# Sigmoid attention with a SiLU MLP behind it: PSUM as three double tiles and two single banks in the stages that run attention under out products

## The chip, the cores and the metric

The kernel runs on one core of a Trainium2 chip. Its engines work side by side, each through its own list of instructions in order: TensorE (PE; its weight loads are listed apart as PEld), VectorE (DVE), ScalarE (ACT), GpSimd (POOL) and SyncE (SP, which here only issues transfers). They wait for each other through semaphores. Matrix products land in PSUM, eight banks of 512 float32 values in each of 128 partitions. The metric is the device time of one execution in microseconds.

## The reference

```python
def _attn_ref(q, k, v):                      # (8, 12, 448, 64) each
    S = q.shape[2]
    scale = 1.0 / np.sqrt(q.shape[-1])
    scores = scale * np.matmul(q, k.transpose(0, 1, 3, 2)) - np.log(S)
    attn = 1.0 / (1.0 + np.exp(-scores))
    return np.matmul(attn, v).astype(np.float32)

def _moe_ref(x, w_in, w_out):                # x (3584, 768), w_in (768, 2048), w_out (2048, 768)
    h = x @ w_in
    g = h * (1.0 / (1.0 + np.exp(-h)))
    return (g @ w_out).astype(np.float32)

def reference(**kwargs):
...
    attn_out = _attn_ref(**attn_kwargs)
    B, H, S, D = attn_out.shape
    x = np.ascontiguousarray(attn_out.transpose(0, 2, 1, 3)).reshape(B * S, H * D)
    return _moe_ref(x=x, **moe_kwargs)
```

The attention is a sigmoid of each score, with no sum over a row, so the scores of one piece of keys can be used as soon as they are there.

## The kernel before

**Attention.** A group g is two pairs of heads of one batch element; there are three groups to a batch element (NQ = 3) and 24 in all. A unit is one seventh of a group's keys (NCH = 7). `scores` (L209) makes one unit: eight half products (L216) into a PSUM tile psc of two banks, from the pool "double", and one ACT sigmoid over both banks (L223) into attnT in SBUF. `values` (L231) multiplies the seven attnT of a group with v (L245) into two banks pav, and DVE scales them into xT (L256). xT is the input of the first product of the MLP.

**First product, h.** For the first pair of batch elements `h_unit` (L273) makes h directly. For the later pairs `h_pair` (L348) makes it by seven products in place of eight of half the size (L364, tiles pa, pb, pc, pd), with sums that DVE and ACT make; the results go through SiLU on ACT (L358) into gTr. The sums of xT that it needs are made by `x_sums` (L334, four DVE subtractions L341 to L344), two thirds of them behind the fifth whole group of a stage (`after_values`, L646).

**Second product, out.** `out_set` (L473) makes the rows of two blocks with seven products po of eight matmuls each (L490), one bank each. DVE reads each po once or twice into the output rows osb (L500 to L525), and makes the sums S between them. `sets` (L556) strings the out_sets of one pair m together and yields after each matmul.

**Stages.** The loop over m (L747, m = 0, 1, 2) has two parts. In the first, attention of the next pair of batch elements runs under the out products of pair m: `burst` (L722) makes two units, and `values` of a group if one is waiting; then some matmuls of po follow, `many` behind a burst of scores alone, `few` (2 for m = 0 and 2, 4 for m = 1) behind one with values. m = 0 and 2 have three out_sets for 21 bursts, m = 1 has four. 14 po matmuls stand ahead of the bursts, and the last 8 behind them. In the second part `h_pair` makes h of the pair whose attention is now there. Ahead of the loop the first two batch elements go through attention and `h_unit`; behind it the last four out_sets run alone.

The order is written out by hand: each engine runs its instructions in the order in which the program calls them, on PE psc, psc, pav, po and so on.

**PSUM.** In the attention parts the eight banks are two pools: two tiles of two banks ("double", for psc) and four of one ("single", for everything else, pav and po among them). A pool hands out its tiles in turn, and a new tile waits until the work on the one that had its place is done. In h_pair every bank is a tile of its own, taken in the order of `ring` (L74): the singles first, longest idle ahead, then the banks of the doubles. `banks_for_attention` (L65) and `banks_for_h` (L74) switch between the two.

Of the kernel before, what the change touches and what calls it, by code (L numbers as in the profile page):

```python
# [11 lines left out]
F32 = mybir.dt.float32  # L12
# [5 lines left out]
def kernel(  # L18
# [14 lines left out]
    P = 128  # L33
# [19 lines left out]
    ctx.enter_context(tc.manual_schedule())  # L53

    psum = ctx.enter_context(ExitStack())
    banks, taken = {}, []
    NBANK, NDOUBLE = 8, 2
    NSINGLE = NBANK - 2 * NDOUBLE

    def new_pool(name, bufs):  # L60
        banks[name] = psum.enter_context(
            tc.tile_pool(name=name, bufs=bufs, space=bass.MemoryType.PSUM, reuse_waits="tile")
        )

    def banks_for_attention():  # L65
        psum.close()
        banks.clear()
        taken.clear()
        new_pool("double", NDOUBLE)
        new_pool("single", NSINGLE)  # L70

    ring = []

    def banks_for_h():  # L74
        oldest = len(taken) % NSINGLE
        ring[:] = [2 * NDOUBLE + (oldest + i) % NSINGLE for i in range(NSINGLE)]
        ring.extend(range(2 * NDOUBLE))
        psum.close()
        banks.clear()
        new_pool("any", 1)  # L80
        for i in range(NBANK):
            banks[i] = banks["any"].tile([P, 512], F32, tag=f"any{i}", name=f"any{i}")

    def one_bank(name):
        if "any" in banks:
            ring.append(ring.pop(0))
            return banks["any"].tile([P, 512], F32, tag=f"any{ring[-1]}", name=name)
        taken.append(name)
        return banks["single"].tile([P, 512], F32, tag="single", name=name)

    banks_for_attention()

# [113 lines left out]

    def scores(g, ch):  # L209
        attnT[g, ch] = p12.tile([P, 2, S], F16, tag="attnT", name="attnT")  # L210
        psc = banks["double"].tile([P, 2, 512], F32, tag="double", name="psc")
        for half in range(2):
            own = slice(half * HP, (half + 1) * HP)
            for j in range(2):
                rows = slice(j * D, (j + 1) * D)
                nc.tensor.matmul(  # L216
                    psc[own, j, :S],
                    qkT["k", g][rows, ch, own],
                    qkT["q", g][rows, :, own],
                    start=True,  # L220
                    stop=True,
                )
        nc.scalar.activation(attnT[g, ch], psc[:, :, :S], AF.Sigmoid, bias=bias_s, scale=QKSCALE)  # L223
# [5 lines left out]
    part_of = {}  # L229

    def values(g, end=NCH):  # L231
        b, iq = divmod(g, NQ)
        if b not in xT:
            assert b < 2 or b - 2 in h_done
            xT[b] = p2.tile([P, NPAIR, S], F16, tag="xT", name="xT")
        pav, done_rounds = part_of.pop(g, None) or (
            [one_bank("pav") for _ in range(2)],
            0,
        )
        for ch in range(done_rounds, end):  # L240
            at = attnT.pop((g, ch))
            for half in range(2):
                own = slice(half * HP, (half + 1) * HP)
                for j in range(2):
                    nc.tensor.matmul(  # L245
                        pav[half][j * D : (j + 1) * D, :S],
                        flat["v", g][own, j, ch, :],
                        at[own, j, :],
                        start=(ch == 0),
                        stop=(ch == NCH - 1),  # L250
                    )
        if end < NCH:
            part_of[g] = pav, end
            return
        for half in range(2):
            nc.vector.tensor_scalar_mul(xT[b][:, half * NQ + iq, :], pav[half][:, :S], SX)  # L256
        if iq == NQ - 1:
            ready.add(b)
# [75 lines left out]
    def x_sums(m, lo, hi):  # L334
        if lo == 0:
            for i in (1, 2, 4):
                tx[m, i] = room_x()
        of = slice(lo, hi)
        x0, x1 = ([xT[2 * m + j][:, c * NQ : (c + 1) * NQ] for c in range(2)] for j in range(2))
        sub = nc.vector.tensor_sub  # L340
        sub(tx[m, 1][:, of], x1[0][:, of], x0[0][:, of])  # L341
        sub(tx[m, 2][:, of], x1[1][:, of], tx[m, 1][:, of])
        sub(x1[0][:, of], x1[1][:, of], x1[0][:, of])
        sub(tx[m, 4][:, of], x0[1][:, of], tx[m, 2][:, of])  # L344
# [211 lines left out]
    def sets(m):  # L556
        for g in range(0, NCH - 1, 2):
            step = out_set(
                block(m, g), row_blocks(m, g), block(m, g + 1), row_blocks(m, g + 1)
            )  # L560
            for i, ns in enumerate(step):
                if m == 0 and g == 0 and i in (10, 14):
                    next(sums)
                if m == 0 and g == 0 and i in (20, 28, 36, 44):
                    next(in_sums)
                yield ns
        if m % 2 == 1:
            g = NCH - 1
            yield from out_set(
                kept, row_blocks(m - 1, g), block(m, g), row_blocks(m, g), m == B // 2 - 1  # L570
            )
# [3 lines left out]
    def rows_if_any(before, copy):  # L575
        if later and later[0][0] < before:
            g, name = later.pop(0)
            dma_transpose(g, name, copy)
            if name == "q":
                behind_rows(g, before)  # L580
# [48 lines left out]
    def after_values(g):  # L629
        if g == 0:  # L630
            load("v", 3)
            load_w_in(2)
            load_w_in(3)
        elif g == 1:
            load("v", 4)
            load_w_out(0, 0)
            load_w_out(0, 1)
        elif g == 2:
            load("v", 5)
            load_w_out(1, 0)  # L640
            load_w_out(1, 1)
            load("kq", 6)
            load("kq", 7)
        elif g + 3 < NQB:
            load("v", g + 3)
        if g >= 2 * NQ and g % (2 * NQ) == 2 * NQ - 2:  # L646
            x_sums(g // (2 * NQ), 0, NQ - 1)

    def values_if_any():
        if waiting:  # L650
            g = waiting.pop(0)
            values(g)
            after_values(g)
            return True
        return False
# [15 lines left out]
    def rounds(g, end):  # L671
        values(g, end)
        if end == NCH:
            after_values(g)
# [47 lines left out]
    def burst(n):  # L722

        new = units[n : n + 2]
        for u in new:
            scores(*u)
        with_values = values_if_any()
        for g, ch in new:
            if ch == NCH - 1:
                waiting.append(g)  # L730
                if 9 <= g + 3 < NQB:
                    later.extend(((g + 3, "k"), (g + 3, "q")))
        return with_values
# [11 lines left out]

    ENDING, FIRST_DENSE = 8, 14
    for m in range(B // 2 - 1):  # L747
        if m > 0:
            banks_for_attention()
        nc.scalar.activation(warm, bias_s, AF.Sigmoid)  # L750
        stream = sets(m)
        for _ in range(FIRST_DENSE):
            next(stream)

        dense = (3 + m % 2) * 7 * NHC - FIRST_DENSE - ENDING
        with_values = 2 * NQ - 1
        few = 2 + 2 * (m % 2)
        many = (dense - with_values * few) / (NT_B - with_values)
        own = 2 * NQ * (m + 2)
        behind_burst = 0.0  # L760
        for n in range(2 * NT_B * (m + 1), 2 * NT_B * (m + 2), 2):
            behind_burst += few if burst(n) else many
            rows_if_any(own, nc.vector.tensor_copy)
            half = int(behind_burst) // 2
            for i in range(int(behind_burst)):
                next(stream)
                if i == half:
                    rows_if_any(own, nc.vector.tensor_copy)
            behind_burst -= int(behind_burst)
        nc.scalar.activation(warm, bias_s, AF.Silu)  # L770
        for _ in stream:
            pass
        (g,) = waiting
        waiting.clear()
        banks_for_h()
        values(g, NCH - 1)

        def last_values():
            values(g)
            after_values(g)  # L780
            x_sums(m + 1, NQ - 1, NQ)
            nc.gpsimd.tensor_copy(gate, tx[m + 1, 4][:1, NQ - 1, :1])

        for i, _ in enumerate(h_pair(m + 1, last_values)):
            if i % 8 == 7:
                rows_if_any(NQB, nc.gpsimd.tensor_copy)
    banks_for_attention()
    for _ in sets(B // 2 - 1):
        pass

# [29 lines left out]
```

## Time and profile before

| | us |
|---|---|
| median of 3 runs | 375.46 (375.2 to 375.9) |
| the profiled execution | 375.68 |
| its span, first to last instruction | 373.7 |

| engine | busy us | share of the span | instructions |
|---|---|---|---|
| PE | 363.9 | 97% | 3009 |
| PEld | 182.4 | 49% | 3009 |
| DVE | 252.2 | 67% | 458 |
| ACT | 251.3 | 67% | 339 |
| POOL | 77.4 | 21% | 116 |

| stage of the loop | from, us | to, us |
|---|---|---|
| m = 0, attention under out products | 76.0 | 125.6 |
| m = 0, h_pair | 125.6 | 160.7 |
| m = 1, attention under out products | 160.7 | 215.5 |
| m = 1, h_pair | 215.5 | 250.6 |
| m = 2, attention under out products | 250.6 | 298.8 |
| m = 2, h_pair | 298.8 | 332.6 |

Times of the trace count from the first instruction. A row in order of time has the start, the time that the row covers, the engine, the line, the operation, what it writes and reads, and how many instructions were merged; in square brackets stands how long the engine was idle before, and what it waited for. Rows of one line that follow each other are merged, and matmuls overlap, so the time of a row is from its first start to its last end. A stage table has, after its bounds, its length, and then each engine's busy time and number of instructions.

### The profile page before, as it was taken

What the parts mean: (1) busy time and instruction counts of PE and PEld (TensorE: products, weight loads), DVE (VectorE), ACT (ScalarE), POOL (GpSimd) and SP (SyncE); (2) the same over time, 40 slices, a digit from 0 to 9 for tenths busy, and PEclk for the clock granted to TensorE, in tenths of its full rate; (3) what the DMA queues carried; (4) which work ended last, traced back from release to release, by engine and by line L of the source; (5) the groups of instructions that cost most, each with busy time, mean ns of one, the idle gap of its engine ahead of it and who ended that gap; (6) DMA issues with size and microseconds to landing.
All of it is one profiled execution on the core that took longest, in us unless ns stands there. A gap on an engine that the chain in (4) does not pass through costs nothing.

```text
span 373.7 us, 7596 instructions
## 1 busy us (share of the span) xinstructions
PE 363.9 (97%) x3009; PEld 182.4 (49%) x3009; DVE 252.2 (67%) x458; ACT 251.3 (67%) x339; POOL 77.4 (21%) x116
## 2 busy tenths in 40 slices
PE   7999999999999999999999999999999999999995
PEld 3554445544444455544444545544444545555553
DVE  2565469867655687867575758795655768797763
ACT  5998885479888756687777846679888946650000
POOL 8566521040051072000014046000100000000000
PEclk9999999999999999999999999999999999999999
DMA  8999999996769599008579669921964030003333
GB/s 133 201 204 204 204 204 204 166 142 128 124 107 210 117 129 172 18 0 128 107 137 165 142 129 134 109 37 28 171 97 97 2 87 0 3 0 84 86 84 84
DMA packets 65698, 42.78 MB, mean 114 GB/s; under 512 B 36096, under 2 KB 62208, under 8 KB 65664
## 3 DMA queue, kind: packets, MB, share of 16 engines
q0 software_dynamic: 27072, 22.58, 42.3%
q1 hardware_dynamic: 38240, 19.44, 27.1%
q8 instruction: 23, 0.38, 0.4%
q10 hardware_dynamic: 352, 0.30, 0.2%
q14 instruction: 11, 0.09, 0.1%
HBM read 45.61 MB, written 11.01 MB: 152 GB/s over the span
## 4 chain that ended last, share of the span: by engine, by line
PE 79%; DMA 9%; ACT 6%; issue 2%; DVE 2%; POOL 0%; ACTq 0%
PE po L490 31%; PE psc L216 9%; PE pa L364 7%; PE pav L245 7%; PE pc L364 7%; PE pd L364 7%; ACT attnT L223 5%; PE ph L277 5%; DMA kf<-in_k_dram 5%; PE pb L364 4%; DMA qf<-in_q_dram 2%; DMA w_in_sb<-in_moe_w_in_dram 2%; PE pw L174 2%; ACT gTr L358 1%; PE ptrq L187 1%
## 5 line engine op out<-in xcount | busy, mean ns | idle before, releaser
L223 ACT ACTIVATE attnT<-psc,bias_s 128x896 f16<-128x896 f32 x168 | 159.2, 1009 | 25.9 <-PE psc L216 25.5
L490 PEld LDWEIGHTS <-S 128*128 128x128 f16 x448 | 40.8, 98 | 36.3 <-issue 10.0
L216 PE MATMUL psc<-qT,kT 64*64 64x448 f16 x672 | 54.8, 364 | 3.0 <-ACT attnT L223 1.8
L256 DVE TENSOR_SCALAR xT<-pav 128x448 f16<-128x448 f32 x48 | 27.7, 620 | 32.5 <-PE pav L245 32.5
L115 POOL DMA_DIRECT2D vf<-in_v_dram x24 | 17.2, 716 | 135.6 <-PE pav L245 131.4
L490 PEld LDWEIGHTS <-gTr 128*128 128x128 f16 x336 | 30.8, 98 | 27.7 <-issue 9.7
L490 PE MATMUL po<-w_out_sb,gTr 128*128 128x384 f16 x224 | 42.5, 327 | 0.1
L490 PE MATMUL po<-T,S 128*128 128x384 f16 x224 | 42.5, 327 | 0.0
L364 PEld LDWEIGHTS <-w_in_sb 128*128 128x128 f16 x288 | 27.7, 98 | 26.9 <-issue 1.7
L490 PE MATMUL po<-w_out_sb,S 128*128 128x384 f16 x224 | 40.4, 327 | 0.0
L245 PE MATMUL pav<-attnT,vf 64*64 64x448 f16 x672 | 39.1, 350 | 0.5 <-DVE gTr L292 0.4
L277 PE MATMUL ph<-xT,w_in_sb 128*128 128x448 f16 x192 | 38.7, 353 | 0.1
L216 PEld LDWEIGHTS <-kT 64*64 64x64 f16 x672 | 17.9, 104 | 35.8 <-issue 32.2
L364 PE MATMUL pa<-xT,w_in_sb 128*128 128x448 f16 x144 | 33.2, 353 | 0.0
L364 PEld LDWEIGHTS <-SI 128*128 128x128 f16 x216 | 21.1, 98 | 20.0 <-issue 0.5
L245 PEld LDWEIGHTS <-vf 64*64 64x64 f16 x672 | 21.8, 106 | 12.8 <-issue 4.7
L277 PEld LDWEIGHTS <-w_in_sb 128*128 128x128 f16 x192 | 17.8, 98 | 19.1 <-issue 3.7
L380 ACT ACTIVATE part<-pa 128x448 f32<-128x448 f32 x24 | 13.1, 544 | 20.1 <-PE pa L364 19.2
L490 PE MATMUL po<-T,gTr 128*128 128x384 f16 x112 | 22.2, 327 | 0.0
L358 ACT ACTIVATE gTr<-pc 128x448 f16<-128x448 f32 x24 | 13.1, 544 | 12.9 <-DVE pc L374 12.5
L374 DVE TENSOR_TENSOR part<-pb,part 128x448 f32<-128x448 f32 x24 | 14.9, 621 | 8.3 <-ACT part L380 5.0
L177 ACT ACTIVATE m<-po 128x384 f32<-128x384 f32 x1 | 0.5, 492 | 27.7 <-PE po L490 27.7
(76 smaller groups left out, 468.4 us busy)
## 6 DMA issues: line engine op xcount, KB each, us to landing
out_dram<-osb SPq DMA_DIRECT2D x54, 192.0 KB, 3.0
vf<-in_v_dram POOLq DMA_DIRECT2D x24, 224.0 KB, 6.7
kf<-in_k_dram POOLq DMA_DIRECT2D x23, 224.0 KB, 7.6
qf<-in_q_dram POOLq DMA_DIRECT2D x23, 224.0 KB, 8.1
w_in_sb<-in_moe_w_in_dram POOLq DMA_DIRECT2D x16, 192.0 KB, 8.1
w_out_sb<-in_moe_w_out_dram POOLq DMA_DIRECT2D x4, 768.0 KB, 14.8
kT<-kr SPq DMA_TRANSPOSE x18, 4.1
qT<-qr SPq DMA_TRANSPOSE x18, 4.4
```

Source lines behind the costliest of these rows:

```text
L115: nc.gpsimd.dma_start(flat[name, g][:, :, c0:c1].rearrange("p i c d -> p i (c d)"), rows_in(name, g)[:, :, c0 * D : c1 * D],)
L174: nc.tensor.matmul(pw, dummy[:, :P], dummy, start=True, stop=True)
L216: nc.tensor.matmul(psc[own, j, :S], qkT["k", g][rows, ch, own], qkT["q", g][rows, :, own], start=True, stop=True,)
L223: nc.scalar.activation(attnT[g, ch], psc[:, :, :S], AF.Sigmoid, bias=bias_s, scale=QKSCALE)
L245: nc.tensor.matmul(pav[half][j * D : (j + 1) * D, :S], flat["v", g][own, j, ch, :], at[own, j, :], start=(ch == 0), stop=(ch == NCH - 1),)
L256: nc.vector.tensor_scalar_mul(xT[b][:, half * NQ + iq, :], pav[half][:, :S], SX)
L277: nc.tensor.matmul(ph[:, :S], w_in_sb[:, cc, fc * P : (fc + 1) * P], xT[b][:, cc, :], start=(at == 0), stop=(at == NCC - 1),)
L358: nc.scalar.activation(gTr[:, r * NG + i, col + c * S : col + (c + 1) * S], h, AF.Silu, bias=0.0, scale=ISX)
L364: nc.tensor.matmul(to, w[:, n, i * P : (i + 1) * P], x[:, n], start=(start and n == 0), skip_group_check=not start, stop=(n == NQ - 1),)
L374: nc.vector.tensor_add(o, po, x)
L380: nc.scalar.activation(got[i, 1], bank[i, "a"], AF.Copy)
L490: nc.tensor.matmul(po[:, :NO2], a[:, fc, :], w[:, fc, :], start=(fc == 0), stop=(fc == NHC - 1))
```

## The change

In the attention parts of the loop over m there are now three double tiles and two single banks. psc and pav take doubles, pav as the two banks of one; po takes the two singles. Ahead of the loop and behind it the split stays at two and four. At m = 0 the pools are now opened anew, which they were not. The ring of h_pair begins with the banks of the double that is longest idle, then come the two singles, then the other two doubles.

```diff
-    banks, taken = {}, []
-    NBANK, NDOUBLE = 8, 2
-    NSINGLE = NBANK - 2 * NDOUBLE
+    NBANK = 8
+    banks, taken, bufs_of = {}, {}, {}
...
-    def banks_for_attention():
+    def banks_for_attention(doubles):
         psum.close()
         banks.clear()
-        taken.clear()
-        new_pool("double", NDOUBLE)
-        new_pool("single", NSINGLE)
+        bufs_of.update(double=doubles, single=NBANK - 2 * doubles)
+        for name, bufs in bufs_of.items():
+            taken[name] = 0
+            new_pool(name, bufs)
+
+    def longest_idle(name):
+        bufs = bufs_of[name]
+        return [(taken[name] + i) % bufs for i in range(bufs)]
 
     ring = []
 
     def banks_for_h():
-        oldest = len(taken) % NSINGLE
-        ring[:] = [2 * NDOUBLE + (oldest + i) % NSINGLE for i in range(NSINGLE)]
-        ring.extend(range(2 * NDOUBLE))
+        doubles = [[2 * i, 2 * i + 1] for i in longest_idle("double")]
+        ring[:] = sum(doubles[:-2], [])
+        ring.extend(2 * bufs_of["double"] + i for i in longest_idle("single"))
+        ring.extend(sum(doubles[-2:], []))
         psum.close()
         banks.clear()
         new_pool("any", 1)
...
-        taken.append(name)
+        taken["single"] += 1
         return banks["single"].tile([P, 512], F32, tag="single", name=name)
 
-    banks_for_attention()
+    def two_banks(name):
+        taken["double"] += 1
+        return banks["double"].tile([P, 2, 512], F32, tag="double", name=name)
+
+    banks_for_attention(2)
...
     def scores(g, ch):
         attnT[g, ch] = p12.tile([P, 2, S], F16, tag="attnT", name="attnT")
-        psc = banks["double"].tile([P, 2, 512], F32, tag="double", name="psc")
+        psc = two_banks("psc")
...
-        pav, done_rounds = part_of.pop(g, None) or (
-            [one_bank("pav") for _ in range(2)],
-            0,
-        )
+        pav, done_rounds = part_of.pop(g, None) or (None, 0)
+        if pav is None and bufs_of["double"] > 2 and "any" not in banks:
+            both = two_banks("pav")
+            pav = [both[:, half] for half in range(2)]
+        elif pav is None:
+            pav = [one_bank("pav") for _ in range(2)]
...
     for m in range(B // 2 - 1):
-        if m > 0:
-            banks_for_attention()
+        banks_for_attention(3)
         nc.scalar.activation(warm, bias_s, AF.Sigmoid)
...
-    banks_for_attention()
+    banks_for_attention(2)
     for _ in sets(B // 2 - 1):
         pass
```

## The prediction

> **What bounds the kernel now.** I read the page first, then stage tables, then each engine's order of time inside three stages.
>
> ```profile
> span 373.7 us, 7596 instructions
> PE 363.9 (97%) x3009; PEld 182.4 (49%) x3009; DVE 252.2 (67%) x458; ACT 251.3 (67%) x339; POOL 77.4 (21%) x116
> L223 ACT ACTIVATE attnT<-psc,bias_s 128x896 f16<-128x896 f32 x168 | 159.2, 1009 | 25.9 <-PE psc L216 25.5
> ```
>
> PE has work in 97% of the span, by the next tables at full clock (1.00); nothing else is near it. ACT mostly waits for PE (25.5 us). So only time in which PE itself is held counts, and it hides well: a psc matmul that is held still overlaps the end of the one before. I therefore split the kernel into stages. The change acts in the attention stages of the loop over m, from the first po of a stage's sets to its last values, roughly: 76.0 to 125.6 (m=0), 160.7 to 215.5 (m=1), 250.6 to 298.8 (m=2). The first two fences are stage tables, of all instructions and of psc's alone (there without PEld, DVE and POOL); the third is PE's only wait inside the stage m=0.
>
> ```profile
> core 0: us, PE busy (x) PEld busy (x) DVE busy (x) ACT busy (x) POOL busy (x), PEclk, DMA share, GB/s
> 76.00:125.60 49.60, 48.76 (x482) 23.38 (x479) 32.75 (x60) 43.38 (x47) 11.06 (x17) 1.00 0.84 139
> 160.70:215.50 54.80, 54.80 (x524) 26.52 (x523) 36.34 (x67) 42.87 (x46) 8.04 (x12) 1.00 0.66 116
> 250.60:298.80 48.20, 47.36 (x468) 22.67 (x467) 30.08 (x55) 42.75 (x45) 2.15 (x3) 1.00 0.42 77
> ```
>
> ```profile
> 76.00:125.60 49.60, 13.93 (x168) 40.04 (x42) 1.00 0.84 139
> 160.70:215.50 54.80, 12.02 (x168) 40.04 (x42) 1.00 0.66 116
> 250.60:298.80 48.20, 13.93 (x168) 40.03 (x42) 1.00 0.42 77
> ```
>
> ```profile
> PE psc L216 <- ACT attnT L223: 0.6, 4, 0.2
> ```
>
> The same 168 psc matmuls take 12.02 us in m=1 but 13.93 in m=0 and m=2, and in m=0 PE idles 0.6 us more before them; m=2 has the same idle time (48.20 - 47.36 = 0.84, as 49.60 - 48.76). So PE is held by 1.91 + 0.6 = about 2.5 us in each of m=0 and m=2, and not at all in m=1. The order of time shows where:
>
> ```profile
> 100.14 0.57 PE L216 MATMUL psc<-qT,kT 64*64 64x448 f16 x8
> ...
> 102.05 0.38 PE L216 MATMUL psc<-qT,kT 64*64 64x448 f16 x4
> 102.59 0.38 PE L216 MATMUL psc<-qT,kT 64*64 64x448 f16 x4 [0.16 <-ACT attnT L223]
> 102.78 0.38 PE L245 MATMUL pav<-attnT,vf 64*64 64x448 f16 x4
> ```
>
> ```profile
> 108.83 0.73 PE L216 MATMUL psc<-qT,kT 64*64 64x448 f16 x8
> ```
>
> ```profile
> 100.64 3.81 ACT L223 ACTIVATE attnT<-psc,bias_s 128x896 f16<-128x896 f32 x4 [0.51 <-PE psc L216]
> ```
>
> A free burst of two psc tiles takes 0.57 us, one tile 0.38, so the second starts 0.2 after the first. At 102.05 it starts 0.54 after it, because with two double tiles it needs the ACT pass of the tile just before the burst (100.64 + half of 3.81 = 102.55). That is 0.34 us of PE lost; at 108.83 it is 0.73 - 0.57 = 0.16. The 2.5 us are made of such holds.
>
> **The change part by part.** Every engine keeps its instructions and their order: the built program of the changed kernel differs only in which earlier instruction a tile waits for (and in two bare waits on PE). Five edits of waits have a cost.
>
> (1) psc rotates over three double tiles, so a burst's second tile needs the ACT pass one further back, which is over when PE arrives (in the rows above: the one that ended at 100.64 + a quarter of 3.81 = 101.6, not 102.55). All the holds go: -2.5 us in m=0, -2.5 in m=2, 0 in m=1. ACT can follow: it is busy 43.38 of 49.60 us, and starts each run of passes after idling for psc (0.51 at 100.64).
>
> [...] Going by PE's idle time before psc alone, this part would be worth 2 x 0.6 us and the whole change would come out at a loss of over 1; by the comparison of stages it is 2 x 2.5. [...]
>
> (2) pav now lies in a double tile, the one that psc used last before the burst. So pav needs the ACT pass that psc's second tile needed before. In the burst at 102.05 that pass has moved with the PE stream by some d, PE itself by d + 0.34: it reaches pav at 102.78 - 0.34 - d = 102.44 - d and may start at 102.55 + 0.05 - d = 102.60 - d (0.05 being the handover from ACT to PE, 102.59 less 102.55 rounded). So 0.16 comes back. The stage has five values calls in bursts; only the psc ahead of two (102.05, 108.83) are held noticeably, and at the second no more than its 0.16 can come back: I give back 0.3 a stage. Bounds: 0, and all that was won at those two, 0.34 + 0.16 = 0.5.
>
> (3) The third double is free for psc again when DVE has moved both halves of pav (1.16 us in the row of 119.62 below). psc asks for it two bursts later, over 2 us after pav's end: nothing while that gap stands; a DVE that is late by more would hold psc by the excess.
>
> (4) po has two single banks instead of four, so a product waits for DVE's pass over the product before the last. Behind most products DVE passes are short against the 8 matmuls between, 0.162 us each ((2.76 - 0.33) / 15 in the row of 122.89 below); the tightest place that I found leaves 0.07 us:
>
> ```profile
> 185.93 0.55 DVE L521 TENSOR_TENSOR osb<-po,osb 128x384 f32<-128x384 f32 x1
> ```
>
> ```profile
> 186.55 0.33 PE L490 MATMUL po<-w_out_sb,gTr 128*128 128x384 f16 x1
> ```
>
> Near the end of each stage it isn't so. After the last whole values, DVE does two xT passes and the four sums of x_sums (L341 to L344) before it comes to po. DVE, then PE, in m=0:
>
> ```profile
> 119.62 1.16 DVE L256 TENSOR_SCALAR xT<-pav 128x448 f16<-128x448 f32 x2 [1.51 <-PE pav L245]
> 120.70 0.61 DVE L341 TENSOR_TENSOR tx<-xT 128x896 f16<-128x896 f16 x1
> ...
> 122.42 0.62 DVE L344 TENSOR_TENSOR tx<-xT,tx 128x896 f16<-128x896 f16 x1
> 122.96 0.55 DVE L514 TENSOR_TENSOR osb<-po,osb 128x384 f32<-128x384 f32 x1
> ```
>
> ```profile
> 122.40 0.38 PE L216 MATMUL psc<-qT,kT 64*64 64x448 f16 x4 [0.16 <-ACT attnT L223]
> ```
>
> ```profile
> 122.89 2.76 PE L490 MATMUL po<-w_out_sb,S 128*128 128x384 f16 x16
> ```
>
> The product that starts at 122.89 will need the bank which L514 leaves at 122.96 + 0.55 = 123.51: with 0.05 of handover it starts 0.67 us later than now, counted against pav, which drives this DVE chain. The last hold of psc (122.40, worth 0.34 like the one at 102.59) lies behind pav and so only lengthens this wait: it wins nothing. Behind the waiting matmul stand the rest of the stage's po, the last values and h_pair, all on PE: nothing covers the wait. m=2 shows the same (296.22 + 0.55 + 0.05 - 296.15 = 0.67):
>
> ```profile
> 296.15 2.11 PE L490 MATMUL po<-w_out_sb,S 128*128 128x384 f16 x12
> ```
>
> ```profile
> 296.22 0.55 DVE L514 TENSOR_TENSOR osb<-po,osb 128x384 f32<-128x384 f32 x1
> ```
>
> In m=1 the chain meets an earlier product, which needs the bank that L510 leaves:
>
> ```profile
> 211.95 0.55 DVE L510 TENSOR_TENSOR osb<-po,m 128x384 f32<-128x384 f32 x1
> ```
>
> ```profile
> 210.91 0.81 PE L490 MATMUL po<-T,gTr 128*128 128x384 f16 x4
> ```
>
> 211.95 + 0.55 + 0.05 - 210.91 = 1.64 us. After the wait DVE finds work ready and catches up before the next product needs it, so it is paid once a stage: +0.67, +1.64, +0.67 = +2.98. Bounds: 0.62, 1.59 and 0.62 without a handover; 0.3 more each if the next product waits as well.
>
> (5) At the change from h_pair to the sets (160.7, 250.6) the banks lie otherwise. Now the second po lands on the bank of the last pd, which ACT still reads:
>
> ```profile
> 159.95 1.04 PE L490 MATMUL po<-w_out_sb,gTr 128*128 128x384 f16 x4
> 160.07 0.54 ACT L358 ACTIVATE gTr<-pd 128x448 f16<-128x448 f32 x1
> 160.67 0.10 PEld L490 LDWEIGHTS <-gTr 128*128 128x128 f16 x1 [0.30 <-issue]
> ```
>
> ```profile
> 249.88 1.04 PE L490 MATMUL po<-w_out_sb,gTr 128*128 128x384 f16 x4
> ```
>
> Four matmuls should take 3 x 0.162 + 0.33 = 0.82, not 1.04. In the changed kernel the first two po take banks 6 and 7, read by ACT passes that ended before; psc takes the later ones, a microsecond afterwards. 0.22 us goes, twice (249.88 has the same 1.04): -0.44. The extra pool opened at m=0 waits only for reads of ph that are over.
>
> The sum: stage m=0: -2.5 + 0.34 + 0.3 + 0.67 = -1.19; m=2 the same; m=1: +1.64; handovers -0.44. Together 2 x -1.19 + 1.64 - 0.44 = **-1.18 us**. It is made against the profiled execution, 375.68 us (its span of 373.7 and 1.98 around it), which gives 374.5. That execution lies 0.22 above the median of the runs, 375.46; from the median the sum gives 374.3, my forecast.
>
> **The rivals.** (A) The holds of psc come back, and the change is slower. Place: values. If ACT's passes don't start earlier when psc does, pav waits for what psc waited for, and each stage keeps only what its first bursts win ahead of the first values, two holds of 0.3; from there on every gain of (1) returns. Then 2 x (-0.6 + 0.67) + 1.64 - 0.44 = +1.3: 376.8. It is slower from the point where a stage keeps less than 1.27 us ((2.98 - 0.44) / 2) of its 2.5. For it: ACT is busy 87% of m=0. Against: it idled for psc in front of that very run of passes (0.51 at 100.64).
>
> (B) The waits on po don't come, because PE is held elsewhere or DVE does its passes sooner than I think; then 2 x (-2.5 + 0.3) - 0.44 = -4.84: 370.6. Against it stands that DVE's work in front of L514 follows pav without a gap.
>
> (C) Gains and losses cancel: one more hold of 0.3 to 0.6 a stage, such as a second po wait in (4), for which the 0.07 at 186.55 speaks, makes -1.18 into about -0.3: 375.2. Against it, DVE idles before most po passes.
>
> (D) The wait of 1.64 lets the clock fall. After the last matmuls the granted clock does fall within the final stretch:
>
> ```profile
> 369.00:373.70 4.70, 0.51 (x4) 0.10 (x1) 0.83 (x2) 0.00 (x0) 0.00 (x0) 0.81 0.47 126
> ```
>
> ```profile
> 1.46 4.02 PE pw L174 x9
> ```
>
> At the start nine 128x512 matmuls take 4.02 us, 0.45 each, where 0.162 for 384 columns gives 0.22: so a fall costs some 2 us, and -1.18 becomes +0.8: 376.3. [...] Here the holds of 0.34 left the granted clock at 1.00 in every stage, so little speaks for it.
>
> **How the numbers follow.** Forecast 0.63; A 0.12; B 0.05; C 0.17; D 0.03. This kernel's measurements can tell about 0.2%, 0.75 us, from no change. The forecast's own range: (2) between 0 and 0.5 a stage, (4) with its bounds, so from 2 x (-2.5 + 0.34 + 0.62) + 1.59 - 0.44 = -1.9 to 2 x (-2.5 + 0.34 + 0.5 + 0.97) + 1.94 - 0.44 = +0.1, and mostly beyond -0.75: I put 0.56 of its 0.63 there, 0.06 within and 0.01 above. With B that makes faster 0.61; C adds to the same, 0.06 + 0.17 = 0.23, and A, D and the rest are slower, 0.16. The range leaves out B below and A and D above, 0.2 in all, and gives the forecast and C half a microsecond more than their bounds: 372.9 to 376.1.
>
> **What would show it.** psc's busy time in m=0 and m=2 falls to about 12.0 us, with no idle before it; pav of some values waits for attnT by 0.1 to 0.2. One wait of po for DVE appears near the end of each stage, about 1.0 us long in m=0 and m=2 (0.67 and the swallowed 0.34) and 1.64 in m=1. Stage m=1 gets longer by 1.6, the two others shorter by about 1.2, h_pair and the last sets stay. I am wrong if pav's waits reach 0.3 in every values (A), if no PE wait on DVE shows (B), if more than one does in a stage (C), or if the clock row drops below 9 (D).

## The result, and the profile after

| | us |
|---|---|
| changed kernel, median of 5 runs | 373.87 (373.35 to 374.36) |
| kernel before, median of 5 runs beside them | 375.35 (374.99 to 375.9) |
| ratio | 0.996, 95% interval 0.9946 to 0.9975 |
| profiled execution of the changed kernel | 374.06, span 372.1 |

The change makes the kernel 1.5 us (0.4%) faster; the prediction said 1.2. The line numbers move by 9 to 11: psc is L225, attnT L232, pav L256, xT L267, the sums of x_sums L352 to L355, po L501.

The stage tables of the changed kernel come first, with the same columns as before: all instructions, then psc's alone (PE and ACT). The bounds have moved with the work: each stage begins with the same matmul as before, and m = 1 ends later by what its wait costs.

```profile
75.90:124.10 48.20, 47.32 (x481) 22.46 (x479) 32.65 (x60) 43.52 (x47) 11.44 (x17) 1.00 0.90 143
159.00:215.40 56.40, 54.91 (x525) 26.29 (x523) 36.54 (x67) 42.88 (x47) 8.07 (x12) 1.00 0.62 112
250.30:297.10 46.80, 45.93 (x469) 21.61 (x467) 30.21 (x55) 43.01 (x47) 2.14 (x3) 1.00 0.46 79
```

```profile
75.90:124.10 48.20, 12.03 (x168) 40.00 (x42) 1.00 0.90 143
159.00:215.40 56.40, 12.02 (x168) 39.98 (x42) 1.00 0.62 112
250.30:297.10 46.80, 12.02 (x168) 39.96 (x42) 1.00 0.46 79
```

psc now takes 12.0 us in all three stages: the holds of m = 0 and m = 2 are gone. These two stages are 1.4 us shorter (49.60 to 48.20, 48.20 to 46.80), and m = 1 is 1.6 us longer (54.80 to 56.40). The two h_pair stages behind m = 0 and m = 1 have lost 0.2 us each (35.1 to 34.9, from the same tables between the bounds).

The waits of PE from 75 to 300 us, in the changed kernel, and then in the kernel before:

```profile
PE po L501 <- DVE osb L525: 1.8, 2, 0.9
PE po L501 <- DVE osb L521: 1.5, 1, 1.5
```

```profile
PE psc L216 <- ACT attnT L223: 1.3, 8, 0.2
```

One kind has taken the place of the other: eight idle times of 0.2 us for ACT have become three longer ones for DVE, one a stage. (These are idle times; what is held but overlaps the matmul before does not show in them: of the 0.34 us at 102.59 in the kernel before they show 0.16.) Where they stand, in order of time, PE and then DVE of the changed kernel in m = 0:

```profile
119.68 0.57 PE L225 MATMUL psc<-qT,kT 64*64 64x448 f16 x8
120.18 0.34 PE L501 MATMUL po<-T,gTr 128*128 128x384 f16 x1
121.39 2.76 PE L501 MATMUL po<-w_out_sb,S 128*128 128x384 f16 x16 [0.88 <-DVE osb L525]
```

```profile
117.45 1.16 DVE L267 TENSOR_SCALAR xT<-pav 128x448 f16<-128x448 f32 x2 [1.50 <-PE pav L256]
118.53 0.62 DVE L352 TENSOR_TENSOR tx<-xT 128x896 f16<-128x896 f16 x1
...
120.25 0.62 DVE L355 TENSOR_TENSOR tx<-xT,tx 128x896 f16<-128x896 f16 x1
120.79 0.55 DVE L525 TENSOR_TENSOR osb<-po,osb 128x384 f32<-128x384 f32 x1
```

The psc burst is free (0.57), and then PE stands until DVE, coming straight from the sums, leaves the bank at 120.79 + 0.55 = 121.34; PE goes on 0.05 later. From the start of the matmul at 120.18 to the next are 1.21 us where 0.17 stood before: 1.04 us more. In m = 1:

```profile
208.04 1.31 PE L501 MATMUL po<-T,S 128*128 128x384 f16 x7
210.84 0.81 PE L501 MATMUL po<-T,gTr 128*128 128x384 f16 x4 [1.49 <-DVE osb L521]
```

```profile
210.23 0.55 DVE L521 TENSOR_TENSOR osb<-po,m 128x384 f32<-128x384 f32 x1
```

The smaller price, of pav in a double, and then the handover, the change from h_pair to the out products:

```profile
100.63 0.57 PE L225 MATMUL psc<-qT,kT 64*64 64x448 f16 x8
101.17 1.52 PE L256 MATMUL pav<-attnT,vf 64*64 64x448 f16 x28
```

```profile
157.64 1.30 PE L501 MATMUL po<-w_out_sb,gTr 128*128 128x384 f16 x7
```

pav starts 0.54 us behind psc, where two free psc tiles take about 0.40 (86.24 to 86.64): it waits 0.14 us. At 157.64 seven po follow each other at 0.162 us ((1.30 - 0.33) / 6), with no wait for ACT.

### The profile page after: what moved, and what is told of

Its sections match the earlier page's. It is cut to its first block, busy times and chain, and to the rows that moved or that the text cites. A ratio compares the mean times of both kernels' runs of the same rounds, so it can differ in the third digit from the quotient of the medians.

```text
span 372.1 us, 7598 instructions
## 1 busy us (share of the span) xinstructions
PE 360.6 (97%) x3009; PEld 179.8 (48%) x3009; DVE 252.0 (68%) x458; ACT 250.9 (67%) x339; POOL 77.5 (21%) x116
## 5 line engine op out<-in xcount | busy, mean ns | idle before, releaser
L232 ACT ACTIVATE attnT<-psc,bias_s 128x896 f16<-128x896 f32 x168 | 159.1, 1007 | 23.4 <-PE psc L225 22.9
L501 PEld LDWEIGHTS <-S 128*128 128x128 f16 x448 | 40.8, 98 | 39.6 <-issue 13.5
L225 PE MATMUL psc<-qT,kT 64*64 64x448 f16 x672 | 50.9, 362 | 1.5 <-ACT qT L186 0.6
L267 DVE TENSOR_SCALAR xT<-pav 128x448 f16<-128x448 f32 x48 | 27.7, 619 | 32.0 <-PE pav L256 32.0
L501 PEld LDWEIGHTS <-gTr 128*128 128x128 f16 x336 | 30.8, 98 | 30.2 <-issue 12.2
L501 PE MATMUL po<-T,S 128*128 128x384 f16 x224 | 42.5, 327 | 0.0
L501 PE MATMUL po<-w_out_sb,gTr 128*128 128x384 f16 x224 | 42.2, 327 | 0.0
L501 PE MATMUL po<-w_out_sb,S 128*128 128x384 f16 x224 | 40.4, 326 | 1.8 <-DVE osb L525 1.8
L256 PE MATMUL pav<-attnT,vf 64*64 64x448 f16 x672 | 38.9, 351 | 0.4 <-DVE gTr L303 0.4
L225 PEld LDWEIGHTS <-kT 64*64 64x64 f16 x672 | 15.4, 104 | 29.3 <-issue 25.7
L256 PEld LDWEIGHTS <-vf 64*64 64x64 f16 x672 | 21.4, 106 | 14.0 <-issue 5.4
L501 PE MATMUL po<-T,gTr 128*128 128x384 f16 x112 | 22.2, 327 | 1.5 <-DVE osb L521 1.5
```

Source lines behind the costliest of these rows:

```text
L225: nc.tensor.matmul(psc[own, j, :S], qkT["k", g][rows, ch, own], qkT["q", g][rows, :, own], start=True, stop=True,)
L256: nc.tensor.matmul(pav[half][j * D : (j + 1) * D, :S], flat["v", g][own, j, ch, :], at[own, j, :], start=(ch == 0), stop=(ch == NCH - 1),)
L501: nc.tensor.matmul(po[:, :NO2], a[:, fc, :], w[:, fc, :], start=(fc == 0), stop=(fc == NHC - 1))
```

## The experiments

Each median stands beside that of the kernel before in the same series, 375.58 for e1 to e4 and 375.67 for e5, e7 and e8; the changed kernel is 1.48 us under the one before in its own. Names and lines in the diffs are those of the changed kernel, or of the kernel before in e5.

### e3: two doubles for psc, one for pav alone

```diff
             taken[name] = 0
-            new_pool(name, bufs)
+            new_pool(name, bufs - (doubles > 2 and name == "double"))
+            if doubles > 2 and name == "double":
+                new_pool("apart", 1)
...
-            both = two_banks("pav")
+            both = banks["apart"].tile([P, 2, 512], F32, tag="apart", name="pav")
```

The ring of h_pair begins with the banks of the double that is apart.

> The changed kernel with the three doubles split for good: two for psc, the third for pav alone; po keeps the two singles. Theory (the win is psc's third tile): psc is held again as before, 2.5 us in m=0 and in m=2, while the po waits stay (0.67, 1.64, 0.67) and the two handovers stay won (0.44): 2.5 us more than the kernel before, 377.9. Rival (the win is that pav no longer shares the singles with po): about the time of the changed kernel, 373.9.

Measured: 378.25 us, ratio 1.0073 (1.0061 to 1.0085), 2.67 us above the kernel before. PE's waits from 75 to 300 us:

```profile
PE po L505 <- DVE osb L525: 1.5, 1, 1.5
PE psc L229 <- ACT attnT L236: 1.3, 8, 0.2
PE po L505 <- DVE osb L529: 1.0, 2, 0.5
```

The holds of psc are back, exactly as before, and the waits on DVE stay. Between the starts of the same matmuls in this trace and that of before there are five differences over 0.04 us in the loop: +0.69, +1.65, +0.69 at the ends of the stages and -0.23 twice at the handovers. This is the change without its gain: two banks for po cost 3.0 us, the handovers give back 0.47. The win comes from psc's third tile alone; giving pav banks of its own wins nothing.

### e2: the sums of x_sums one at a time, behind po passes

```diff
     def after_values(g):
...
-            x_sums(g // (2 * NQ), 0, NQ - 1)
+            due_sums.extend(x_sums(g // (2 * NQ), 0, NQ - 1))
...
+    def next_sum():
+        if due_sums:
+            do, *what = due_sums.pop(0)
+            do(*what)
...
         po = yield from product(sg[2], tw[3])
         add(c22, po, c12)
+        next_sum()
```

x_sums returns its four subtractions instead of making them; next_sum stands behind DVE's pass over each of the seven po of out_set, and what is left is made ahead of h_pair.

> The changed kernel with the four subtractions of x_sums (lines 341 to 344 of before) no longer in one block behind values, but one at a time, each behind the next DVE pass over a po. Theory (PE waits near each stage's end because that block stands on DVE ahead of the po passes): the waits of 1.04, 1.66 and 1.04 us go, so 3.7 us less than the changed kernel, 370.1; up to 0.5 more than that if a later po pass comes late. Rival (two banks for po are too few whatever DVE does): within 0.5 us of 373.9, with the waits at other products.

Measured: 370.13 us, ratio 0.9855 (0.984 to 0.9869). Between 75 and 300 us PE no longer idles at any wait (pav's two waits of 0.14 a stage stay, hidden under the matmul before). By the starts of the same matmuls the loop is 3.70 us shorter than in the changed kernel, as expected. DVE's order at the end of m = 0 shows why:

```profile
116.92 1.16 DVE L267 TENSOR_SCALAR xT<-pav 128x448 f16<-128x448 f32 x2 [1.50 <-PE pav L256]
118.11 0.56 DVE L537 TENSOR_TENSOR osb<-po,osb 128x384 f32<-128x384 f32 x1
118.59 0.62 DVE L364 TENSOR_TENSOR tx<-xT 128x896 f16<-128x896 f16 x1
120.02 0.55 DVE L541 TENSOR_TENSOR osb<-osb,po 128x384 f32<-128x384 f32 x1 [0.82 <-PE po L510]
120.49 0.62 DVE L364 TENSOR_TENSOR tx<-xT,tx 128x896 f16<-128x896 f16 x1
```

The po pass now comes right behind xT, 1.19 us behind its start, where it was 3.34 (120.79 less 117.45 above). The same DVE work is done in the time in which it used to idle for PE (the 0.82 and others). So two banks for po are enough, once DVE reads them in time; this version is 1.4% faster than the kernel before, and the fastest that was found.

### e5: the same late sums in the kernel before

> The kernel before (two doubles, four singles throughout) with the subtractions of x_sums one at a time behind po passes, as in e2. Theory (with four singles PE does not wait there, so the place of that block costs nothing): within 0.3 us of the kernel before, 375.4. Rival (the late block costs the kernel before too, and e2 won something that has nothing to do with the banks): 1 us or more below it, 374.4 or less.

The edit is that of e2. Measured: 375.69 us, ratio 1.0002 (0.9994 to 1.0011). No start of a matmul in the loop has moved by over 0.04 us between the two traces. With four singles the block of sums cost nothing, and moving it wins nothing. What e2 won, it won from the waits that the split into three and two had made.

### e4: one more DVE pass in the block

```diff
         sub(tx[m, 1][:, of], x1[0][:, of], x0[0][:, of])
+        if lo == 0:
+            sub(tx[m, 1][:, of], x1[0][:, of], x0[0][:, of])
```

> The changed kernel with one subtraction of x_sums made twice (line 341 of before, the same result) in the block behind the fifth group: one more DVE pass of 0.55 us a stage ahead of the po pass. Theory (that chain on DVE sets when PE goes on): 0.55 to 0.65 us more in each of three stages, 1.65 to 1.95 more than the changed kernel, 375.5 to 375.8. Rival (DVE has room there, PE waits for something else): 373.9, no change.

Measured: 376.11 us, ratio 1.0029 (1.0014 to 1.0043), 0.53 above the kernel before and so 2.0 above the changed kernel, against 1.65 to 1.95 expected. The waits themselves grew by 0.66, 0.65 and 0.66 us (starts of the same matmuls in both traces). The repeated pass costs somewhat more than 0.55: the passes around it, each of which touches the tile that the one ahead has just written, start 0.65 us apart (118.09, 118.74, 119.40 in e4's trace), the later ones of the block 0.54. So what is put on DVE between the last xT and the po pass is paid by PE in full, here and with the two passes of e8 (1.31 us).

### e1 and e7: two doubles in m = 1

```diff
     for m in range(B // 2 - 1):
-        banks_for_attention(3)
+        banks_for_attention(2 if m == 1 else 3)
```

> The changed kernel with the split of before (two doubles, four singles) in stage m=1 alone. Theory (the third double wins only in m=0 and m=2, and m=1 only pays the po wait near its end): 1.64 us less than the changed kernel, up to 0.23 of it lost again if the po at 160.7 waits for ACT as before, so 372.2 to 372.5. Rival (the third double also helps m=1, unseen): 373.9 or more.

Measured: 374.16 us, ratio 0.9962 (0.995 to 0.9974): 1.42 under the kernel before, as the changed kernel. The expectation missed. PE's waits from 75 to 300 us, and the place of one in order of time:

```profile
PE po L501 <- DVE osb L525: 1.8, 2, 0.9
PE po L501 <- ACT gTr L369: 1.5, 2, 0.7
```

```profile
157.07 0.73 PE L375 MATMUL pd<-xT,SI 128*128 128x448 f16 x3
158.53 1.14 PE L501 MATMUL po<-w_out_sb,gTr 128*128 128x384 f16 x6 [0.73 <-ACT gTr L369]
```

The wait of m = 1 is gone, as said, but two others have come: the first po behind each h_pair waits for ACT, 0.90 us from start to start each (1.085 and 1.084 where 0.189 stood). When the split changes from stage to stage, the first single lies on another bank than h_pair left longest idle. The expectation counted only the second po of the handover (0.23), not the first. e7 lays the singles first in both splits:

```diff
-        bufs_of.update(double=doubles, single=NBANK - 2 * doubles)
+        bufs_of.clear()
+        bufs_of.update(single=NBANK - 2 * doubles, double=doubles)
...
-        doubles = [[2 * i, 2 * i + 1] for i in longest_idle("double")]
+        at = bufs_of["single"]
+        doubles = [[at + 2 * i, at + 2 * i + 1] for i in longest_idle("double")]
...
-        ring.extend(2 * bufs_of["double"] + i for i in longest_idle("single"))
+        ring.extend(longest_idle("single"))
```

> As e1 (two doubles in m=1, three in m=0 and m=2), but the singles take the first banks in both splits and the doubles those behind, so that the first po behind each h_pair takes a bank that was free for long. Theory (e1 missed because the first po at 159.1 and 249.1 landed on a bank that ACT still read, 0.9 us each): these two waits go, 1.65 us less than the changed kernel, 372.2. Rival (a change of the split between stages costs by itself): 374.0 as e1.

Measured: 372.47 us, ratio 0.9912 (0.9899 to 0.9925), 3.2 under the kernel before: 1.7 better than the changed kernel, as expected. Only the waits at the ends of m = 0 and m = 2 are left:

```profile
PE po L503 <- DVE osb L527: 1.7, 2, 0.9
```

### e8: two more DVE passes in m = 1 alone

```diff
         sub(tx[m, 1][:, of], x1[0][:, of], x0[0][:, of])
+        if lo == 0 and m == 2:
+            for _ in range(2):
+                sub(tx[m, 1][:, of], x1[0][:, of], x0[0][:, of])
```

(In x_sums m is the pair whose h comes next, so m == 2 is the stage m = 1.)

> The changed kernel with line 341 of before made three times in place of once, in stage m=1 alone: PE's wait near the end of that stage grows from 1.65 to about 2.95 us. Theory (e4's wait of 2.3 us let the clock fall in some executions, 1 to 3 us each): 1.3 us more where the clock holds, 375.2, and 1 to 3 more where it falls, now in most executions, so 376 to 378 with a granted clock under 0.995. Rival (the low clock of e4 was another disturbance): 375.2 in all of them.

The reason for it is in e4's trace: behind its wait in m = 1, which had grown to 2.15 us of idle time, PE ran at half rate for a while:

```profile
211.72 0.81 PE L503 MATMUL po<-T,gTr 128*128 128x384 f16 x4 [2.15 <-DVE osb L523]
...
214.04 4.02 PE L503 MATMUL po<-w_out_sb,S 128*128 128x384 f16 x16
```

The sixteen po of 214.04 take 4.02 us, where the sixteen of 121.39 in the changed kernel take 2.76. The stage table of e4 around it (the column behind POOL is the granted clock):

```profile
208.00:212.00 4.00, 1.85 (x17) 0.89 (x10) 3.93 (x8) 1.91 (x2) 0.10 (x1) 1.00 0.47 60
212.00:216.00 4.00, 4.00 (x23) 1.67 (x21) 1.28 (x3) 3.03 (x3) 0.00 (x0) 0.65 0.00 0
216.00:220.00 4.00, 4.00 (x39) 1.96 (x38) 1.58 (x3) 0.36 (x2) 0.00 (x0) 0.93 0.38 95
```

e8, with 2.81 us of idle time there, shows the same in its profiled execution:

```profile
212.32 1.44 PE L504 MATMUL po<-T,gTr 128*128 128x384 f16 x4 [2.81 <-DVE osb L524]
```

```profile
212.00:216.00 4.00, 3.68 (x19) 1.38 (x19) 1.50 (x4) 1.61 (x2) 0.00 (x0) 0.58 0.00 0
216.00:220.00 4.00, 4.00 (x42) 2.08 (x41) 1.96 (x4) 1.78 (x3) 0.00 (x0) 1.00 0.28 69
```

Measured: 376.43 us, ratio 1.0019 (1.0002 to 1.0036). The 11 executions fall into two groups: four at 375.12 to 375.38 with a mean granted clock of 0.997 to 1.0, seven at 376.32 to 378.57 with 0.993 to 0.995. e4's 12 do as well: eight at 376.04 to 376.17 (0.997 to 1.0), four at 377.1 to 379.15 (0.993). So the expectation holds for most executions, and the rival falls: the low clock comes back. Seven of 11 against four of 12 fits a longer wait that makes the clock fall more often, but is too few to show it: a split as uneven comes by chance about one time in five, and the two series ran on different chips. In the two profiled executions the half rate cost 1.7 us (e4) and 1.4 us (e8), by the starts of the same matmuls. The slow groups lie 1.0 to 3.3 us above the quick ones; why 379.15 and 378.57 took so much longer than others with the same mean clock is open. For the executions without a profile only the mean clock is on record, not where it fell. The changed kernel, with 1.49 us of idle time, has a mean clock of 0.997 to 0.999 in its five executions; in its trace the clock first falls at 371.00, behind the last matmul.

## Why the prediction was right

- **(1), psc's third tile.** Forecast 2.5 us of holds gone in each of m = 0 and m = 2, none in m = 1. Measured: psc at 12.0 us everywhere, and no wait for ACT in front of it. Counted by the starts of the same matmuls, each of the two stages wins 2.7 us so, before pav's waits are taken off. The 0.2 more is the start of the po that follow a held psc, which also came 0.02 us later, eight times in m = 0; the comparison of stage tables does not see it. Over the two stages this is nearly all of the 0.37 us by which the loop's gain, counted below, exceeds the sum. e3 shows that the third tile is what won it.
- **(2), pav's wait.** Forecast two waits of 0.15 a stage. Measured: two in m = 0 and two in m = 2, 0.14 each.
- **(3), pav's double free in time.** No wait of psc for DVE shows. The margin itself was not tried.
- **(4), po on two singles.** Forecast 0.67, 1.64 and 0.67, and about 1.0 where the last hold of psc is swallowed. Measured 1.04, 1.66 and 1.04, and 0.69, 1.65 and 0.69 in e3, where the holds are back and nothing is swallowed. That DVE's block of sums sets them is shown from both sides, by e2 and by e4. The place with 0.07 us to spare did hold; with the handover of 0.05, which the prediction left out there, it had only 0.02.
- **(5), the handovers.** Forecast 0.22 twice, measured 0.23 twice. That it hangs on which bank a po gets, e1 and e7 show on the first po.

The sum was -1.18 us; the two profiled executions differ by 1.62, of which the loop's stages and handovers make 2 x -1.37 + 1.66 - 0.47 = -1.55 by their starts. The mechanism was right term by term; what was a little too small is the gain of (1).

Of the rivals, A fell: ACT's passes did start earlier with psc (the run of four at 100.64 now starts at 99.22), and pav's waits stayed at 0.14. B fell with the waits seen, though e2 shows what it would have been worth: all the gain without the loss. C's second po wait did not come. D did not happen in the changed kernel, but its mechanism is there: e4 needs only 0.66 us more of the same wait to show it. Its price of 2 us was read off the first matmuls; the record of the clock begins behind them, at 6.65 us with full clock, so that a low clock ahead of it was argued and not read. That a fall doubles the time of a matmul, as this price assumed, e4 shows (0.320 us for 0.162); the two falls seen cost 1.7 and 1.4 us.

## What to carry to other kernels

Banks given to one tile are taken from another, and the bill comes at the one place where the engine that reads the poorer tile is late; so list, for each tile that loses a buffer, the gap between its reader's end and the next writer, over the whole stage, and look at what stands on the reader's queue where that gap is negative. If it is work that nothing needs yet, move it behind the reads: here this gave back the 3.7 us that the two banks had cost (e2), and nothing in the kernel that had four (e5). And when pools are opened again in another split, check which bank the first tile lands on and who still reads it.

## What the runs showed of the hardware that was not expected

The granted clock of PE fell in some executions, and not in others, of the same kernel. In the profiled execution of e4 it fell behind an idle time of 2.15 us, in that of e8 at one of 2.81 us; by the mean clock it fell in 4 of 12 executions of e4 and in 7 of 11 of e8. PE then ran at half rate: in e4's trace po follow each other at 0.320 us instead of 0.162. In e4 PE had run at full rate again for 1.5 us when the clock fell (211.72 to 213.18); in e8 it fell 0.34 us before PE went on (211.98 to 212.32). In both it stayed low for 3.41 us and was full again then.

The record of the clock that each trace keeps shows more. In all nine traces every change lies a whole number of times 3.413 us behind the first one recorded, which is to full clock (in e4 61 times, from 4.96 to 213.18; in e8 60 times, from 7.18 to 211.98; 107 times in the kernel before, from 6.65 to 371.87, and in the changed kernel, from 5.78 to 371.00). Stage tables cut at these times, first e4, then e8, then the last work of e7 (PE's busy time stands behind the length, the granted clock behind POOL):

```profile
209.77:213.18 3.41, 1.47 (x14) 0.59 (x14) 2.96 (x6) 0.61 (x2) 0.00 (x0) 1.00 0.31 49
213.18:216.59 3.41, 3.41 (x12) 1.53 (x11) 0.56 (x1) 3.16 (x4) 0.00 (x0) 0.50 0.00 0
```

```profile
208.57:211.98 3.41, 0.94 (x6) 0.46 (x5) 3.31 (x7) 1.53 (x2) 0.00 (x0) 1.00 0.54 67
211.98:215.39 3.41, 3.07 (x15) 1.03 (x15) 1.35 (x3) 1.00 (x2) 0.00 (x0) 0.50 0.00 0
```

```profile
364.70:368.11 3.41, 1.59 (x10) 0.75 (x8) 1.58 (x3) 0.00 (x0) 0.00 (x0) 1.00 0.39 102
368.11:370.50 2.39, 0.00 (x0) 0.00 (x0) 0.00 (x0) 0.00 (x0) 0.00 (x0) 1.00 0.36 102
```

PE idled 1.94 us in e4's stretch ahead of the fall (3.41 - 1.47) and 2.47 in e8's; in e7's it idled 1.82 and no fall followed. These are the nearest on either side: behind the first change, each stretch of the nine traces with 1.94 us of idle time or more is followed by half clock, the ends of the programs among them, and none with 1.82 or less (the ends of matmuls are modelled, so both figures are approximate). So, as far as nine traces show it, a fall goes with the idle time that lies in one stretch: 1.94 us and more against 1.82 and less. That fits a wait of 2.15 us that lets the clock fall in some executions and not in others. The 1.49 us of the changed kernel lie below 1.82 wherever a stretch begins; in its trace at most 1.22 of them fell into one (207.16 to 210.58).
